# q by Strassen's seven products over two heads and two query blocks, in an attention and gMLP kernel of fp32 products in three passes

## The chip, the cores and the metric

The kernel runs on one core of one Trainium2 chip. The metric is the device time of one execution in microseconds (us). It is told as the median of three runs; one further execution was profiled, and its trace is what the views below read. The engines are PE (TensorE, matrix products into PSUM), DVE (VectorE), ACT (ScalarE), POOL (GpSimd) and SP (SyncE, which here issues most DMAs). Each engine takes its own instructions strictly in the order in which the program wrote them.

## The reference

The input x is 2048 rows of 512. It is normalized per row, and the result feeds an attention with 32 heads over the last 512 cached keys and values (no mask), and a gMLP branch whose SiLU gates the attention's output:

```python
xn = _layernorm(x, axis=-1)
s = _A_ref(xn, A_k_cache, A_v_cache, A_wq, A_wo)   # q = xn @ wq, 32 heads of 128
#   scores = q k^T * 128 ** -0.5 ; p = softmax(scores) ; o = p v ; s = o @ wo
g = _silu(_B_ref(xn, B_w_in, B_w_sp, B_b_sp, B_w_out))
#   z = gelu(xn @ w_in); z1, z2 = halves; z2 = layernorm(z2)
#   (z1 * (w_sp @ z2 + b_sp)) @ w_out
return x + s * g
```

All tensors are fp32.

## The kernel before

Every product is made to hold fp32's accuracy by three passes: an operand is split into a part `hi`, rounded to the matrix engine's fp32r format, and the rest `lo` (the operand minus `hi`), and `mm3` adds hi·hi, hi·lo and lo·hi in PSUM. So each operand costs an ACT instruction (the rounding copy) and a subtraction, `rest`, on DVE or POOL. POOL cannot serve where the operand lies in PSUM; there DVE subtracts.

The work stands in one loop over steps `t` (line 372). A block `b` is one head with 512 queries, so there are 128 blocks of 4 steps; one head takes 16 steps. A step works on several blocks at once, at fixed distances:

- `score(t)`: 3 products of 512 columns into one of four PSUM buffers `ps`, then DVE takes the negated row maximum `nm` (line 229), and ACT writes `prob` = exp(score + nm) with its row sums (line 231). The next-but-one score needs the same PSUM buffer again, so PE can run two steps ahead of ACT's exponential.
- `qproj`, 7 steps ahead: q for a later block, 12 products of 512 columns per block, 3 in each step. At the fourth, ACT and DVE split the result into `qT_h` and `qT_l`.
- `turn(t-1)`: DVE transposes `prob` in 32x32 pieces into `pB` (line 239), SP writes it to a DRAM buffer; two steps after a block's last one `turned` reads it back into `pL` in another order, so that p stands transposed.
- `shares(b, c)`, 10 steps behind: ACT rounds a quarter of `pL` into `pT_h` (line 256), POOL makes the rest `pT_l`.
- `pv`, 12 steps behind: 3 products of p and v per step; after four, ACT and DVE split them into `oT_h` and `oT_l`.
- `outp`, 17 steps behind: 3 products with wo, and DVE scales by the row sum and adds to `sacc` (line 283).

Within a step the engines' orders follow the program: `shares` and the splitting of weights come first, then `score`, then the products, then the splits of results, and `turn` last. So on DVE a step reads `nm`, `sacc`, perhaps `qT_l` and `oT_l`, then `pB`; on ACT it reads `pT_h`, perhaps a weight's rounding, the exponential, then perhaps `qT_h` and `oT_h`.

The weights of a head come in four pieces of 128x512 (wq, k, v, wo), loaded 8 steps before `split_piece` splits them with ACT and POOL. The 32 heads are run one after the other, each over all four query blocks; `sacc` holds all 2048 rows of s. The normalized and transposed x stays on chip as hi and lo (`xh`, `xl`). The first half of the gMLP's input product (`z1_piece`, 12 products of 344 columns each, 32 pieces) fills steps at the start and the end of the loop in which the pipeline is not full. After the loop come the gMLP's second half, the spatial product with w_sp and the last projection, which the change leaves as they are but for buffer names and the order of the row tiles.

Of the kernel before, what the change touches and what calls it, by code (L numbers as in the profile page):

```python
# [17 lines left out]
P = 128  # L18
# [15 lines left out]
XL, QL, ML, PL, OL = 11, 7, 10, 12, 17  # L34
Q = 32
# [3 lines left out]
def mixer_kernel(ctx: ExitStack, tc: tile.TileContext, x, wh, w_in, w_sp, b_sp, w_out, out):  # L39
# [35 lines left out]
    xp = ctx.enter_context(tc.tile_pool(name="xp", bufs=4))  # L75
    wp = left.enter_context(tc.tile_pool(name="wp", bufs=2))
    raws = ExitStack()
    rawp = raws.enter_context(tc.tile_pool(name="rawp", bufs=6))
# [4 lines left out]
    zs = att.enter_context(tc.tile_pool(name="zs", bufs=2))  # L83
    sp = att.enter_context(tc.tile_pool(name="sp", bufs=1))
    ap = att.enter_context(tc.tile_pool(name="ap", bufs=2))
    sacc = sp.tile([P, NT, D], F32, name="sacc")

    raw, wt = {}, {}  # L90

    def load_piece(key, k):
        n = 512 if key[0] == "h" else NB
        r = rawp.tile([P, 512], F32, name="raw")
        raw[key, k] = r
        nc.sync.dma_start(r[:, :n], (wh if key[0] == "h" else w_in)[key[1], :, k])
# [11 lines left out]
    FOLLOWS = {("w", 1): (0, 1, 0, 2), ("w", 2): (1, 3, 2, 3), ("w", 3): (0, 1, 0, 2)}  # L108

    def split_piece(key, k, engine, early=False):  # L110
        n = 512 if key[0] == "h" else NB
        if key == ("w", 0):
            hi = ap.tile([P, 512], F32R, name="pT_h", bufs=4)
            lo = ap.tile([P, 512], F32R, name="pT_l", bufs=4)
        else:
            f = FOLLOWS[key][k] if key in FOLLOWS and not early else k
            hi = wp.tile([P, 512], F32R, name=f"wh{f}")
            lo = wp.tile([P, 512], F32R, name=f"wl{f}")
        r = raw.pop((key, k))[:, :n]
        nc.scalar.copy(hi[:, :n], r)  # L120
# [6 lines left out]
    GROUPS = [(a, a + 1) for a in range(4)] + [(a, a + 2) for a in range(4, NT, 2)]  # L127
    mv, rx, xT = {}, {}, {}
# [4 lines left out]
    def ln_stats(i):  # L133
        a, b = next(g for g in GROUPS if g[0] <= i < g[1])
        if i == a:
            mv[a] = stats.tile([P, 2, 2], F32, name="mv", bufs=5)
        stt = stats.tile([P, 6], F32, name="stt", bufs=4)
        nc.vector.bn_stats(stt, sacc[:, i, :])
        nc.vector.bn_aggr(mv[a][:, i - a, :], stt)
        if i == b - 1:  # L140
            r = stats.tile([P, 2], F32, name="rs_r", bufs=5)
            rsqrt(mv[a][:, :b - a, 1], r, b - a, stats.tile([P, 2], F32, name="rs_t", bufs=4))
            for j in range(a, b):
                rx[j] = mv[a][:, j - a, 0:1], r[:, j - a:j - a + 1]

    def ln_apply(i):
        mean, r = rx[i]
        if i:
            nc.vector.scalar_tensor_tensor(sacc[:, i, :], sacc[:, i, :], mean, r.to_broadcast([P, D]),
                                           op0=OP.subtract, op1=OP.mult)  # L150
        else:
            for k in range(2):
                sl = sacc[:, i, k * (D // 2):(k + 1) * (D // 2)]
                nc.vector.tensor_scalar(sl, sl, mean, r, op0=OP.subtract, op1=OP.mult)

    def ln_flip(i, parts=1):
        g, j = divmod(i, 4)
        if j == 0:
            hi = xp.tile([P, NC, 512], F32R, name="xh")
            lo = xp.tile([P, NC, 512], F32R, name="xl")  # L160
            xT[g] = (hi, lo)
        ps = ps_step.tile([P, NC, P], F32, name="ps_3")
        n, rests = NC // parts, []
        for k in range(parts):
            for c in range(k * n, k * n + n):
                nc.tensor.transpose(ps[:, c, :], sacc[:, i, c * P:(c + 1) * P], ident)  # L166
            hi, lo = (t[:, k * n:k * n + n, j * P:(j + 1) * P] for t in xT[g])
            nc.scalar.copy(hi, ps[:, k * n:k * n + n])
            rests.append((lo, ps[:, k * n:k * n + n], hi))
        return rests if parts > 1 else [rest(nc.vector, *r) for r in rests]  # L170


    def zmm(ps, i, n, cs):
        g, j = divmod(i, 4)
        for c in cs:
            mm3(ps, c == 0, c == NC - 1, tuple(t[:, c, j * P:(j + 1) * P] for t in xT[g]),
                cols(wt[("w", n), c], 0, NB))
# [5 lines left out]
    def zmm_in(order, ps, i, n):  # L183
        g, j = divmod(i, 4)
        for k, (a, b, c) in enumerate(order):
            nc.tensor.matmul(ps, xT[g][a][:, c, j * P:(j + 1) * P], wt[("w", n), c][b][:, :NB],
# [9 lines left out]
    def z1_out(i, n, ps):  # L196
        z = zs.tile([P, 384], F32, name="z1")[:, :NB]
# [8 lines left out]

    def qproj(b, c):
        h, qb = divmod(b, NQ)
        if c == 0:
            qps[b] = ps_acc.tile([P, 512], F32, name="ps_a")  # L210
        mm3(qps[b], c == 0, c == NC - 1, cols(wt[("h", h), 0], c * P, (c + 1) * P), tuple(t[:, c, :] for t in xT[qb]))

    def qproj_out(b, c):
        if c == NC - 1:
            hi = ap.tile([P, 512], F32R, name="qT_h")
            lo = ap.tile([P, 512], F32R, name="qT_l")
            ps = qps.pop(b)
            nc.scalar.activation(hi, ps, AF.Copy, scale=SCALE)
            nc.vector.scalar_tensor_tensor(lo, ps, SCALE, hi.bitcast(F32), op0=OP.mult, op1=OP.subtract)
            qT[b] = (hi, lo)  # L220

    def score(t):
        b, j = divmod(t, 4)
        ps = ps_step.tile([P, W], F32, name="ps_3")
        mm3(ps, True, True, cols(qT[b], j * P, (j + 1) * P), wt[("h", b // NQ), 1])
# [34 lines left out]
    def pv(b, c):  # L260
        if c == 0:
            pps[b] = ps_acc.tile([P, 512], F32, name="ps_a")
        mm3(pps[b], c == 0, c == 3, cols(wt[("h", b // NQ), 2], c * P, (c + 1) * P), pT.pop((b, c)))
# [10 lines left out]
    def outp(b, j):  # L274
        h, qb = divmod(b, NQ)
        i = qb * 4 + j
        ps = ps_step.tile([P, D], F32, name="ps_3")
        mm3(ps, True, True, cols(oT[b], j * P, (j + 1) * P), wt[("h", h), 3])
        rs = sums[b][:, j:j + 1]
        if h == 0:  # L280
            nc.vector.tensor_scalar(sacc[:, i, :], ps, rs, None, op0=OP.mult)  # L281
        else:
            nc.vector.scalar_tensor_tensor(sacc[:, i, :], ps, rs, sacc[:, i, :], op0=OP.mult, op1=OP.add)  # L283
        if h == H - 1:
            nc.sync.dma_start(s_dram[:, i, :], sacc[:, i, :])


    T0, T1, Z1 = -QL, NSTEP + OL, NSTEP - 3
    loads, splits = {}, {}

    def plan(key, k, t):

        loads.setdefault(max(T0, t - 8), []).append((key, k))
        splits.setdefault(t, []).append((key, k))

    for h in range(1, H):
        for k, d in enumerate((-10, -4, 1, 9)):
            plan(("h", h), k, 16 * h + d)
    for k, d in enumerate((-5, 6, 9)):
        splits.setdefault(d, []).append((("h", 0), 1 + k))  # L300
    for n, ds in enumerate(((-12, -9, -7, -4), (1, 4, 13, 17), (17, 17, 17, 17))):
        for k, d in enumerate(ds):
            plan(("w", 1 + n), k, NSTEP + d)
# [7 lines left out]
    load_piece(("h", 0), 0)  # L311
    load_x(4, 8)
    for k in range(1, 4):
        load_piece(("h", 0), k)
    for a in range(8, NT, 4):
        load_x(a, a + 4)
# [12 lines left out]
    ln_stats(0)  # L329
    low0 = split_piece(w0, 0, None), split_piece(w0, 1, None)  # L330
    ln_stats(1)
    ln_apply(0)
# [3 lines left out]
    ln_apply(1)  # L336
    for r in low:
        rest(nc.vector, *r)
    split_piece(w0, 2, nc.vector)
    split_piece(w0, 3, nc.vector)  # L340
# [4 lines left out]
    ln_stats(2)  # L345
# [4 lines left out]
    ln_stats(3)  # L350
# [340 lines left out]
```

## Time and profile before

| | us |
|---|---|
| runs before | 1840.91, 1840.68, 1837.23; median 1840.68 |
| the profiled execution | 1841.09, of which its span 1839.2 |
| loop: score of the first step to that of the last | 45.5 to 1434 (starts, view of `qT_l`'s products) |
| share of the loop in the span | about three quarters |

The span is the time from the first to the last instruction of the trace; 1.9 us lie around it. In the timeline a row has the start in us, the length in us, the engine, the line, the operation, what it writes and reads with shapes, and in brackets how long the engine sat idle ahead of it and who ended that. In the table of windows the columns are the window, its length, then the busy time and the number of instructions of PE, PE's weight loads, DVE, ACT and POOL, then PE's clock, the DMA share and GB/s.

### The profile page before, as it was taken

How to read it: one execution, taken by the hardware profiler on the slowest of the kernel's cores; microseconds unless marked ns; L12 is line 12 of the kernel's file. 1: busy time of each engine (PE TensorE's matmuls, PEld its weight loads, DVE VectorE, ACT ScalarE, POOL GpSimd, SP SyncE). 2: the span in 40 equal slices, each digit the busy share in tenths (PEclk: the TensorE clock that was granted, in tenths of full speed). 3: DMA queues.
4: the chain of work that ended last, by engine and by line, in shares of the span. 5: the costliest groups of instructions: out<-in, count | busy, mean ns of one | idle time of the engine just before them, and what ended most of it. 6: DMA issues, size and time to landing. Idle time of an engine off the chain costs nothing.

```text
span 1839.2 us, 27426 instructions
## 1 busy us (share of the span) xinstructions
PE 1827.4 (99%) x8828; PEld 1573.1 (86%) x8828; DVE 1356.3 (74%) x2268; ACT 1019.4 (55%) x2188; POOL 873.6 (48%) x703
## 2 busy tenths in 40 slices
PE   8999999999999999999999999999999999999999
PEld 7888888888888888888888888888888999999998
DVE  7688888888888888888888888888888566333433
ACT  3566656666666665666666665665666445343422
POOL 3365555565565565555566555565566244000000
PEclk9999999999999999999999999999999999999999
DMA  5698888888888888888888888888888714554532
GB/s 190 179 234 216 217 219 224 215 218 218 221 214 217 216 219 217 216 214 217 219 224 217 218 216 226 215 218 217 218 215 225 222 65 153 174 184 140 182 120 91
DMA packets 404225, 369.69 MB, mean 201 GB/s; under 512 B 23056, under 2 KB 298768, under 8 KB 404080
## 3 DMA queue, kind: packets, MB, share of 16 engines
q1 hardware_dynamic: 399472, 362.30, 75.1%
q10 hardware_dynamic: 4608, 5.64, 0.9%
q8 instruction: 69, 1.13, 0.3%
q14 instruction: 76, 0.62, 0.1%
HBM read 213.70 MB, written 154.14 MB: 200 GB/s over the span
## 4 chain that ended last, share of the span: by engine, by line
PE 96%; DVE 1%; DMA 1%; ACT 1%; issue 0%; POOL 0%; ACTq 0%; SPq 0%; DVEq 0%; POOLq 0%
PE ps_a L61 14%; PE ps_a L62 14%; PE ps_a L63 14%; PE ps L63 13%; PE ps L61 13%; PE ps L62 13%; PE ps_g L61 4%; PE ps_g L62 4%; PE ps_g L63 4%; PE ps_f L63 1%; PE ps_f L62 1%; PE ps_f L61 1%; DMA z_dram<-z 0%; PE ps_f L621 0%; PE ps L166 0%
## 5 line engine op out<-in xcount | busy, mean ns | idle before, releaser
L57 POOL TENSOR_TENSOR pT_l<-pL,pT_h 128x512 fp32r<-128x512 f32 x507 | 658.6, 1299 | 572.1 <-ACT pT_h L256 526.2
L231 ACT ACTIVATE prob<-ps,nm 128x512 f32<-128x512 f32 x512 | 353.4, 690 | 533.6 <-DVE nm L229 531.5
L283 DVE SCALAR_TENSOR_TENSOR sacc<-ps,sums,sacc 128x512 f32<-128x512 f32 x496 | 370.7, 748 | 170.5 <-PE ps L63 170.4
L239 DVE STREAM_TRANSPOSE pB<-prob 128x512 f32<-128x512 f32 x512 | 359.4, 702 | 1.5 <-ACT pT_h L256 0.8
L229 DVE TENSOR_REDUCE nm<-ps 128x1 f32<-128x512 f32 x512 | 334.8, 654 | 3.6 <-PE ps L63 3.6
L256 ACT CAST pT_h<-pL 128x512 fp32r<-128x512 f32 x512 | 315.8, 617 | 7.6 <-ACT z L198 3.4
L61 PE MATMUL ps<-wh,qT_h 128*128 128x512 f32 x512 | 199.9, 390 | 0.9 <-DVE sacc L281 0.9
L63 PE MATMUL ps<-wh,oT_l 128*128 128x512 f32 x512 | 199.3, 389 | 0.3 <-DVE oT_l L57 0.3
L61 PE MATMUL ps_a<-xh,wh 128*128 128x512 f32 x512 | 199.4, 390 | 0.0
L62 PE MATMUL ps_a<-pT_l,wh 128*128 128x512 f32 x512 | 199.3, 389 | 0.0
L62 PE MATMUL ps_a<-xl,wh 128*128 128x512 f32 x512 | 199.3, 389 | 0.0
L62 PE MATMUL ps<-wl,qT_h 128*128 128x512 f32 x512 | 199.3, 389 | 0.0
L63 PE MATMUL ps_a<-xh,wl 128*128 128x512 f32 x512 | 199.2, 389 | 0.0
L63 PE MATMUL ps<-wh,qT_l 128*128 128x512 f32 x512 | 199.2, 389 | 0.0
L62 PE MATMUL ps<-wl,oT_h 128*128 128x512 f32 x512 | 199.2, 389 | 0.0
L61 PE MATMUL ps_a<-pT_h,wh 128*128 128x512 f32 x512 | 199.2, 389 | 0.0
L63 PE MATMUL ps_a<-pT_h,wl 128*128 128x512 f32 x512 | 199.2, 389 | 0.0
L61 PE MATMUL ps<-wh,oT_h 128*128 128x512 f32 x512 | 199.2, 389 | 0.0
L57 POOL TENSOR_TENSOR wl<-raw,wh 128x512 fp32r<-128x512 f32 (+1 forms) x132 | 169.6, 1286 | 37.0 <-ACT wh L120 37.0
L63 PE MATMUL ps_g<-z_h,xl 128*128 128x344 f32 x512 | 161.8, 316 | 0.0
L61 PE MATMUL ps_g<-z_h,xh 128*128 128x344 f32 x512 | 161.8, 316 | 0.0
L62 PE MATMUL ps_g<-z_l,xh 128*128 128x344 f32 x512 | 161.8, 316 | 0.0
(135 smaller groups left out, 2991.4 us busy)
## 6 DMA issues: line engine op xcount, KB each, us to landing
p_dram<-pB SPq DMA_DIRECT2D x512, 256.0 KB, 3.8
pL<-p_dram SPq DMA_DIRECT2D x512, 256.0 KB, 5.8
raw<-wh SPq DMA_DIRECT2D x128, 256.0 KB, 4.4
xh<-w_sp SPq DMA_DIRECT2D x32, 256.0 KB, 5.8
xl<-w_sp SPq DMA_DIRECT2D x28, 256.0 KB, 5.8
u_dram<-uB SPq DMA_DIRECT2D x15, 384.0 KB, 2.3
uL<-u_dram SPq DMA_DIRECT2D x60, 96.0 KB, 2.1
z_dram<-z ACTq DMA_DIRECT2D x32, 172.0 KB, 2.4
```

Source lines behind the costliest of these rows:

```text
L57: engine.tensor_tensor(lo, whole, hi.bitcast(F32), op=OP.subtract)
L61: nc.tensor.matmul(ps, lh, rh, start=first, stop=False)
L62: nc.tensor.matmul(ps, lh, rl, start=False, stop=False)
L63: nc.tensor.matmul(ps, ll, rh, start=False, stop=last)
L229: nc.vector.tensor_reduce(nm, ps, axis=AX.X, op=OP.max, negate=True)
L231: nc.scalar.activation(prob[t], ps, AF.Exp, bias=nm, accum_out=sums[b][:, j:j + 1])
L239: nc.vector.transpose(pB.rearrange("p (k q) -> p k q", q=Q), prob.pop(t))
L256: nc.scalar.copy(h, p)
L283: nc.vector.scalar_tensor_tensor(sacc[:, i, :], ps, rs, sacc[:, i, :], op0=OP.mult, op1=OP.add)
```

## The change

For each pair of heads and pair of query blocks the change computes q by the seven products of Strassen's scheme (in Winograd's form) in place of eight: the two-by-two blocks are (two heads) x (two halves of the 512 inputs) on the weight's side, and (two halves of the inputs) x (two blocks of 512 queries) on x's side. A group `g` is such a pair of pairs: four blocks, 16 steps. Each of its seven products is 6 matmuls of 512 columns, so a group has 42 in place of 48. The first group is computed as before.

What comes with it:

- Four sums of x's blocks per half of the rows ("T1" to "T4") are formed, split into hi and lo, and kept in SBUF beside the original blocks. With them only one half of x fits, so the 32 heads are run twice: first all heads over rows 0 to 1023, then all heads over rows 1024 to 2047 (`where`). `sacc` shrinks to half. k, v and wo are loaded and split twice.
- The first half's sums are made in steps -3 to 1 (`t_sums`, `t_split`). Its original blocks are written to DRAM (`keep_x`) and read back for the stage after the loop. The second half's x is loaded, normalized, transposed, summed, split and written to DRAM in 72 small pieces of work (`later_x`) spread over steps 30 to 207, and fetched as seven blocks of 1 MB (`fetch_x`) while the last group of the first half goes on.
- Per group: two loads of wq, four sums of 128x256 on POOL (`q_sum`), seven splits of 128x256 (`q_split`): ACT rounds each, POOL makes the rest of three, DVE that of four. The products accumulate in three PSUM buffers; ACT evicts three times into `qs`, DVE adds three more results onto these (`q_evict`), and four splits give `qT_h`, `qT_l` (`q_done`): three with ACT and POOL, one with ACT and DVE.
- The z1 pieces stand otherwise: 11 of them in steps -7 to 5 (before: 13 in -7 to 9), and 16 at the end (before: 14).

```diff
+    def q_split(g, k):
+        a11, a12, a21, a22, s1 = q_parts(g)
+        src = (a11, a12, a11, s1, a21, a12, a22)[k]
...
+        nc.scalar.copy(hi, src)
+        rest(nc.gpsimd if k in (0, 1, 5) else nc.vector, lo, src, hi)
...
+    def q_products(g, s):
+        for m in q_span(g, s):
+            k, r = divmod(m, 6)
+            c, v = divmod(r, 3)
+            bank = BANK[k]
...
+            nc.tensor.matmul(qps[g, bank], wt["q", g, k][a][:, c * P:(c + 1) * P], X[g * 2 // H][ORDER[k]][:, b, c],
+                             start=first, stop=r == 5, skip_group_check=True)
+    def q_evict(g, k):
+        ps = qps[g, BANK[k]]
+        if k in (0, 2, 3):
+            t = qps[g, "t", k] = ap.tile([P, 512], F32, name="qs", bufs=3)
+            nc.scalar.activation(t, ps, AF.Copy, scale=SCALE)
+        elif k < 6:
+            t = qps[g, "t", {1: 0, 4: 3, 5: 2}[k]]
+            nc.vector.scalar_tensor_tensor(t, ps, SCALE, t, op0=OP.mult, op1=OP.add)
+    def q_done(g, k):
+        if k == 6:
+            q_out(4 * g + 3, qps[g, "a"], True, nc.vector)
+        else:
+            t, n = {1: (0, 0), 4: (3, 2), 5: (2, 1)}[k]
+            q_out(4 * g + n, qps[g, "t", t], False, nc.gpsimd)
...
+    for h in range(2 * H):
+        for k, d in ((1, -4 if h else -5), (2, 6), (3, 11)):
+            if h:
+                plan(("h", h), k, 8 * h + d)
...
+        t0 = 16 * g - LEAD
+        sums_at, splits_at = (-5, -4, -2, 1), (-3, -1, 2, 4, 6, 7, 10)
...
+    for n, f in enumerate(f for p in range(4) for f in later_x(p)):
+        at(30 + 5 * n // 2, f)
```

In `later_x` each of the four rounds does, in this order: load, statistics of two tiles and two normalizing multiplications on DVE, two transposes on PE with a copy by ACT, four subtractions on POOL, and eight splits of 128x256 of which ACT rounds all, DVE makes the rest of five and POOL that of three; each split is written to DRAM.

DVE in the middle of the loop, before: from one row maximum to the next but two (`oT_l` and `qT_l` are the rests of o and q, `pB` the turned probabilities). Every subtraction here has an operand in PSUM.

```order
L229 TENSOR_REDUCE nm<-ps_8587 128x1
L283 SCALAR_TENSOR_TENSOR sacc<-ps_8601,sums,sacc 128x512
L57 TENSOR_TENSOR oT_l<-ps_a,oT_h 128x512
L239 STREAM_TRANSPOSE pB<-prob 128x512
L229 TENSOR_REDUCE nm<-ps_8621 128x1
L283 SCALAR_TENSOR_TENSOR sacc<-ps_8637,sums,sacc 128x512
L219 SCALAR_TENSOR_TENSOR qT_l<-ps_a,qT_h 128x512
L239 STREAM_TRANSPOSE pB<-prob 128x512
L244 RECIPROCAL sums<-sums 128x4
L229 TENSOR_REDUCE nm<-ps_8654 128x1
```

The same engine with the change, in steps 3 to 6 of a group's products (`x_739` is the ring of split weights, `wq` and `wqs` hold the weights and a sum of them, `qs` the evicted products).

```order
L439 TENSOR_REDUCE nm<-ps_11457 128x1
L494 SCALAR_TENSOR_TENSOR sacc<-ps_11471,sums,sacc 128x512
L449 STREAM_TRANSPOSE pB<-prob 128x512
L59 TENSOR_TENSOR x_739<-wqs,x_739 128x256
L439 TENSOR_REDUCE nm<-ps_11493 128x1
L494 SCALAR_TENSOR_TENSOR sacc<-ps_11507,sums,sacc 128x512
L423 SCALAR_TENSOR_TENSOR qs<-ps_a,qs 128x512
L59 TENSOR_TENSOR oT_l<-ps_a,oT_h 128x512
L449 STREAM_TRANSPOSE pB<-prob 128x512
L439 TENSOR_REDUCE nm<-ps_11526 128x1
L494 SCALAR_TENSOR_TENSOR sacc<-ps_11541,sums,sacc 128x512
L59 TENSOR_TENSOR x_739<-wq,x_739 128x256
```

A subtraction whose two operands both lie in SBUF now stands directly ahead of a row maximum, in four steps of every sixteen.

ACT with the change, from the exponential of step 3 to that of step 6.

```order
L441 ACTIVATE prob,sums<-ps_11457,nm 128x512
L466 CAST pT_h<-pL 128x512
L395 CAST x_739<-wqs 128x256
L441 ACTIVATE prob,sums<-ps_11493,nm 128x512
L480 CAST oT_h<-ps_a 128x512
L466 CAST pT_h<-pL 128x512
L441 ACTIVATE prob,sums<-ps_11526,nm 128x512
L349 CAST qT_h<-qs 128x512
L466 CAST pT_h<-pL 128x512
L395 CAST x_739<-wq 128x256
L441 ACTIVATE prob,sums<-ps_11560,nm 128x512
```

The rounding that DVE's subtraction needs (`x_739`) stands behind the exponential of the step before, the evictions of that step and the rounding of p; before the change, what stood there on ACT beside p was only the rounding of `qT_h`, `oT_h` or of a weight whose rest POOL makes.

More of the change, by code (lines that the diff above doesn't have):

```diff
@@ L274, in outp @@
     def outp(b, j):
-        h, qb = divmod(b, NQ)
+        h, qb = where(b)
         i = qb * 4 + j
+        at = sacc[:, i % T8, :]
         ps = ps_step.tile([P, D], F32, name="ps_3")
@@ L296, in mixer_kernel @@
[L296 to L301, printed above, removed]
-        for k, d in enumerate(ds):
-            plan(("w", 1 + n), k, NSTEP + d)
+        if h % H == 0:
+            nc.vector.tensor_scalar(at, ps, rs, None, op0=OP.mult)
+        else:
+            nc.vector.scalar_tensor_tensor(at, ps, rs, at, op0=OP.mult, op1=OP.add)
@@ L310, in mixer_kernel @@
     load_early(1, [(0, 4)])
-    load_piece(("h", 0), 0)
+    load_piece(("q", 0), 0)
     load_x(4, 8)
[L313 to L316, printed above, removed]
+    load_piece(("h", 0), 1)
+    load_piece(("q", 1), 0)
     ident = const.tile([P, P], F32, name="ident")
@@ L328, in mixer_kernel @@
     w0, w1 = ("w", 0), ("w", 1)
[L329 to L332, printed above, removed]
+    rows = [sacc[:, i, :] for i in range(T8)]
+    ln_open(0)
+    low0 = split_piece(w0, 0, None, True), split_piece(w0, 1, None, True)
+    ln_open(1)
+    ln_apply(rows[0], 0)
     low = ln_flip(0, 2)
@@ L478, in mixer_kernel @@
     SP = (6, 8, 10, 12)
-    for i in range(NT):
+    for pos, i in enumerate(ZO):
         for n in (2, 3):
```

448 lines of the change are left out of this document (320 added, 128 removed).

## The prediction, made before the changed kernel ran

> **What bounds the kernel now.** I read the page's sums first, then the chain that ended last, then a window in the middle of the loop, then the timeline there.
>
> ```profile
> span 1839.2 us, 27426 instructions
> PE 1827.4 (99%) x8828; PEld 1573.1 (86%) x8828; DVE 1356.3 (74%) x2268; ACT 1019.4 (55%) x2188; POOL 873.6 (48%) x703
> PE 96%; DVE 1%; DMA 1%; ACT 1%; issue 0%; POOL 0%; ACTq 0%; SPq 0%; DVEq 0%; POOLq 0%
> 400.00:800.00 400.00, 400.00 (x1767) 331.31 (x1766) 331.79 (x551) 244.33 (x551) 236.11 (x184) 1.00 0.86 218
> ```
>
> PE is busy for 99% and makes 96% of the last chain. In the window DVE is busy for 83%, ACT for 61%, POOL for 59%, with a DMA share of 0.86. The busy PE could still be waiting inside its pipeline, so I look at starts:
>
> ```profile
> 800.16 0.39 PE L61 MATMUL ps<-wh,qT_h 128*128 128x512 f32 x1
> ...
> 800.72 0.74 DVE L283 SCALAR_TENSOR_TENSOR sacc<-ps,sums,sacc 128x512 f32<-128x512 f32 x1
> ...
> 801.38 0.70 DVE L239 STREAM_TRANSPOSE pB<-prob 128x512 f32<-128x512 f32 x1
> ...
> 802.88 0.39 PE L61 MATMUL ps<-wh,qT_h 128*128 128x512 f32 x1
> ```
>
> A step takes 2.72 us for 12 matmuls: 0.2267 us each, though one is shown as 0.39 long. Sixteen steps take 43.5. PE sets the pace; the others have a sixth of the time or more to spare. But PE can run only two steps ahead of the exponential, so what decides after a cut of PE's work is how fast DVE and ACT can go round: row maximum, exponential, further work, next row maximum. The trace shows that once, at the loop's start, where steps are short because `pv` and `outp` have not begun:
>
> ```profile
> 87.57 0.65 DVE L229 TENSOR_REDUCE nm<-ps 128x1 f32<-128x512 f32 x1
> ...
> 88.32 0.69 ACT L231 ACTIVATE prob<-ps,nm 128x512 f32<-128x512 f32 x1 [0.21 <-DVE nm L229]
> ...
> 89.00 0.58 ACT L270 CAST oT_h<-ps_a 128x512 fp32r<-128x512 f32 x1
> ...
> 89.61 0.69 DVE L57 TENSOR_TENSOR oT_l<-ps_a,oT_h 128x512 fp32r<-128x512 f32 x1 [1.38 <-ACT oT_h L270]
> ...
> 90.84 0.65 DVE L229 TENSOR_REDUCE nm<-ps 128x1 f32<-128x512 f32 x1
> ...
> 92.27 0.59 ACT L218 ACTIVATE qT_h<-ps_a 128x512 fp32r<-128x512 f32 x1
> ...
> 92.75 0.62 ACT L256 CAST pT_h<-pL 128x512 fp32r<-128x512 f32 x1
> ...
> 93.25 0.63 ACT L120 CAST wh<-raw 128x512 fp32r<-128x512 f32 x1
> 93.44 1.30 POOL L57 TENSOR_TENSOR pT_l<-pL,pT_h 128x512 fp32r<-128x512 f32 x1 [1.98 <-ACT pT_h L256]
> ...
> 94.18 0.66 DVE L229 TENSOR_REDUCE nm<-ps 128x1 f32<-128x512 f32 x1
> ...
> 95.55 0.50 PE L61 MATMUL ps<-wh,qT_h 128*128 128x512 f32 x1 [0.89 <-DVE sacc L281]
> ...
> 96.03 0.65 DVE L229 TENSOR_REDUCE nm<-ps 128x1 f32<-128x512 f32 x1
> ...
> 97.88 0.65 DVE L229 TENSOR_REDUCE nm<-ps 128x1 f32<-128x512 f32 x1
> ```
>
> Here the round is late and PE waits for it, at 95.55. From one `nm` to the next a late round takes 3.27 us with an `oT` split (87.57 to 90.84), 3.34 with a `qT` split (90.84 to 94.18), 1.85 without (96.03 to 97.88). In the kernel before, sixteen steps hold four of the first, four of the second, eight of the third: 41.2 us, under PE's 43.5. So the round never rules there, with only 5% of room.
>
> **The change part by part.** *PE's work.* 31 groups lose 6 matmuls each: 186 x 0.2267 = 42.2 us. A group's PE time falls from 43.5 to 42.16. Sixteen transposes are added at the start; four take 0.65 us, so 2.6:
>
> ```profile
> 26.92 0.65 PE ps L166 x4
> ```
>
> *The round with the change.* I go through the sixteen steps of a group, `s` = 0 to 15 from its first product, by the rows above. From `nm` to the exponential 0.75 (87.57 to 88.32), from the exponential to ACT's next 0.68 (88.32 to 89.00), then 0.48 for an eviction (92.27 to 92.75) and 0.50 for a rounding of 512 (92.75 to 93.25); the rest on DVE starts 0.03 after its rounding ends (89.00 + 0.58, 89.61). Not shown is a split of 128x256. Its nearest rows:
>
> ```profile
> L120 ACT CAST pT_h<-pL x4: 475/478/482, 4.9 to 9.1; 128x344 fp32r<-128x344 f32 x4
> L57 DVE TENSOR_TENSOR xl<-ps,xh x17: 415/686/693, 9.3 to 58.6; 128x512 fp32r<-128x512 f32 x15, 128x256 fp32r<-128x256 f32 x2
> 1477.12 2.21 DVE L57 TENSOR_TENSOR wl<-raw,wh 128x344 fp32r<-128x344 f32 x5
> ```
>
> Between 0.48 for 344 columns and 0.62 for 512, a rounding of 256 is 0.40. DVE's subtraction of 256 lasts 0.415; of 344 columns five in a row take 0.44 each, so 256 cost 0.35 of DVE's time. An eviction on DVE costs what `sacc` does, 0.66 (800.72 to 801.38). The intervals from `nm` to `nm` when late:
>
> - six plain ones: 11.1; three with `oT`: 9.8; `oT` behind a rounding of `qT_h` (s = 12): 3.27 + 0.50 = 3.77; two with an eviction on DVE (11, 13): 2 x 2.51 = 5.0;
> - 1 to 2, the split of q, then DVE's weight split: 3.34 + 0.35 = 3.7;
> - 3 to 4: 0.75 + 0.68 + 0.50 (p's rounding) + 0.43 + 0.35 = 2.71; 5 to 6 and 9 to 10, with one more instruction on ACT ahead: 3.2 each, 6.4;
> - 2 to 3: eviction, p and a weight piece between two exponentials make ACT later than DVE: 0.4.
>
> Sum 42.9 us. This is above PE's 42.16: the new round replaces PE as what sets the pace, and of 1.36 us per group at most 0.6 are left.
>
> *DVE against POOL.* DVE's four weight splits read two operands from SBUF, which no DVE instruction in the middle of the loop before does. The trace has such a one beside a POOL subtraction:
>
> ```profile
> 1452.06 1.29 POOL L57 TENSOR_TENSOR pT_l<-pL,pT_h 128x512 fp32r<-128x512 f32 x1 [4.96 <-ACT pT_h L256]
> ...
> 1452.40 1.32 DVE L57 TENSOR_TENSOR wl<-raw,wh 128x344 fp32r<-128x344 f32 x1 [1.61 <-ACT wh L120]
> ```
>
> DVE's took 1.32 in place of 0.44 to 0.5, and ended 0.37 after POOL's end: it waited POOL out. In the four steps POOL starts p's subtraction 0.69 after p's rounding (92.75 to 93.44), and DVE becomes ready 0.50 + 0.43 = 0.93 after it. POOL then has 1.05 of 1.29 left: a wait of up to 1.05 at s = 4 and 10, and about 0.55 at s = 2 and 6, where other work delays DVE. Bounds for a group: no wait, 42.9; all waits whole, 46.1. POOL is busy with 25 subtractions of 1.29 and 7 half ones, at some 0.75 (estimated between its 344 and 512 columns, 0.93 and 1.30, in the row below), 37.5 us of every group, so DVE seldom finds it idle, but it may come late in POOL's instruction. I take the middle, 44.5.
>
> ```profile
> L57 POOL TENSOR_TENSOR wl<-raw,wh x132: 927/1300/1307, 34.8 to 1472.8; 128x512 fp32r<-128x512 f32 x127, 128x344 fp32r<-128x344 f32 x5
> ```
>
> The Trainium skill ("SBUF — State Buffer", section "SBUF: two separate sides") calls what DVE and GpSimd share an exclusive lock, held for the whole instruction by whoever starts first, against a DVE op with two SBUF inputs. Taken strictly, each of the four waits is whole and the group is at 46.1, some 48 us more in all than the middle; the row at 1452.40 agrees, but is one case with an otherwise idle POOL.
>
> Over 30 groups (the first one's products lie in the short steps): 30 x (44.5 - 43.5) = +30 us, bounds -18 and +78.
>
> *The second half's x*, in steps 30 to 207. It was made in the start before, where DVE had room; now it stands ahead of `nm` inside the round. Four times: two statistics and two multiplications on DVE, five DVE splits:
>
> ```profile
> L138 DVE BATCH_NORM_STATS2 stt<-sacc x16: 660/684/695, 3.2 to 44.2; 128x6 f32<-128x512 f32 x16
> L149 DVE SCALAR_TENSOR_TENSOR sacc<-sacc,mv,rs_r x15: 720/742/981, 8.7 to 53.7; 128x512 f32<-128x512 f32 x15
> ```
>
> Statistics with their small second step 1.5, multiplications 2 x 0.67, splits between 0.35 and 0.9 more than a plain step, 5 x 0.45: 5.1 us, four times 20. The multiplications and splits have two SBUF operands again; seven waits of 0.6 add up to 17: between 20 and 37, taken 28.
>
> *Start, switch and DMA.* Five steps at the start lose the z1 piece that covered them (12 matmuls of 344, 1.89 us) while the first p is under way; nothing lost or 5 x 1.89 = 9.4, taken 4 with the transposes. At the switch seven loads of 1 MB meet p's traffic:
>
> ```profile
> 15.00:20.00 5.00, 3.46 (x19) 2.88 (x18) 3.88 (x6) 1.01 (x3) 3.87 (x6) 0.90 1.06 396
> pL<-p_dram SPq DMA_DIRECT2D x512, 256.0 KB, 5.8
> ```
>
> At the 396 GB/s of the start's loads 1.05 MB take 2.65 us: seven, at most 18.5 us of delay. But each has two to three steps to itself and p's read lands in 5.8 us, with four steps from its issue to its use: 3 taken. In the loop transfers of 256 KB go from 36 to 40 per group; 0.86 x 40/36 = 0.96 of DMA share at the old pace, 0.93 at the new one: no bound, but little room. Rounding of k, v and wo a second time, and the sums, lie on ACT and POOL between exponentials; what of it is on the round is counted above.
>
> Sum: 1839.2 + 30 + 28 + 4 + 3 = 1904 us of span, with 1.9 around it (the profiled execution's 1841.1 against its span) 1906. The median before lies 0.4 under the profiled execution, which I leave out.
>
> **The rivals.** *PE stays the bound.* The two steps of PE's lead absorb the late rounds, as DVE's mean load would allow (331.8 of 400 now). Then the 42.2 come off, 2.6 and some 10 for start, switch and the x work come on: span 1809, time 1811. For it: PE lost only 0.89 us in the one place shown. Against: the sum of the round, which no lead can shorten. *No meeting with POOL.* DVE comes after POOL's instruction each time: 1839 - 18 + 20 + 7 = 1848, time 1850; against it POOL's 37.5 us of work per group. *Half and half.* PE rules outside the x work (19 groups, 26 gained), the round inside (11 groups at 42.9 and 20 of x work, 13 lost), start and switch 7: 6 gained, time 1835. *DMA becomes the bound*: with 32 writes of 256 KB in short rows and the loads of x the share passes 1 in steps 30 to 207, `pL` lands late, ACT's rounding waits and the exponential behind it. If a tenth is added to those 180 steps (490 us) on top of the forecast: 1955.
>
> **How the numbers follow.** Chances: the forecast 0.47 (its own range 1870 to 1960), PE stays the bound 0.20, no meeting 0.15, half and half 0.12, DMA 0.06. From these: faster 0.24 (the second case and a third of half and half), within 0.2%, about what this measurement can tell from no change, 0.06, slower 0.70. The range must reach into the case of PE's bound and to DMA's: 1812 to 1960 leaves out half of the first, and the ends of the forecast and of DMA, under 0.2 together.
>
> **What would show it.** If the forecast holds, the 16 steps of a group in the second half take 44 to 45.5 us, PE shows gaps ahead of the scores that end on ACT's exponential or on DVE, DVE's `x<-wq` subtractions last about 0.9 on the mean in place of 0.415, and groups in steps 30 to 207 take 2 to 3 us more. PE at 98% or more, groups of 42.2 us and short subtractions would make it wrong; so would POOL or `pL` as the releaser ahead of PE's products, or of ACT's rounding of p.

## The result, and the profile after

| | before | after |
|---|---|---|
| median of 4 runs, us | 1840.22 | 1985.03 (1982.25 to 1987.7) |
| span of the profiled execution, us | 1839.2 | 1982.1 |

The ratio is 1.079, with a 95% interval from 1.077 to 1.081: slower, as forecast, but by 145 us where 66 were forecast, and beyond the range (1812 to 1960). The page's sums and the engines' shares of the chain that ended last, after:

```profile
span 1982.1 us, 28951 instructions
PE 1860.5 (94%) x8658; PEld 1537.5 (78%) x8658; DVE 1484.3 (75%) x2427; ACT 1174.1 (59%) x2627; POOL 1264.1 (64%) x1127
PE 36%; ACT 20%; DVE 17%; DMA 11%; issue 10%; POOL 4%; SPq 1%; ACTq 0%; DVEq 0%; POOLq 0%
```

PE has 170 matmuls fewer in the records and is shown busier than before (1860.5 us for 1827.4), so its busy time does not tell how much it gets done. What tells is the chain: PE fell from 96% to 36%, and ACT and DVE, 1% each before, hold 37%. Two stretches of the table of windows, the first while the second half's x is made, the second behind the switch:

```profile
400.00:800.00 400.00, 361.50 (x1509) 279.87 (x1508) 334.57 (x539) 256.07 (x601) 310.61 (x276) 0.99 0.90 234
1000.00:1400.00 400.00, 385.37 (x1641) 303.55 (x1641) 344.89 (x566) 271.38 (x635) 325.51 (x282) 1.00 0.92 233
```

No engine is full: PE makes 1509 matmuls in the first and 1641 in the second, against 1767 in 400 us before. Its clock is no reason, at 1.00 in the second. What is left is a chain across engines that is full on none. The view of waits says which (us in total, times, longest), first before, then after:

```profile
ACT prob L231 <- DVE nm L229: 531.5, 472, 2.1
...
DVE sacc L283 <- PE ps L63: 170.4, 359, 1.7
```

```profile
ACT prob L441 <- DVE nm L439: 502.7, 328, 7.3
...
PEld ps L63 <- DVE sacc L494: 159.1, 177, 6.5
...
PE ps L63 <- DVE sacc L494: 93.4, 126, 6.1
```

ACT's exponential waits for `nm` in both kernels, before even longer, so this row alone says nothing. What has turned round is PE and DVE: before, DVE's `sacc` waited for PE's product 359 times; now PE's score waits for `sacc`, which DVE makes right behind `nm`. One turn of this round, from the timeline of a steady group, with the rows of other work left out:

```profile
1227.18 0.41 ACT L395 CAST x<-wq 128x256 fp32r<-128x256 f32 x1
1227.49 0.70 DVE L449 STREAM_TRANSPOSE pB<-prob 128x512 f32<-128x512 f32 x1
1228.09 0.75 POOL L386 TENSOR_TENSOR wq<-wq 128x256 f32<-128x256 f32 x1
1228.18 0.95 DVE L59 TENSOR_TENSOR x<-wq,x 128x256 fp32r<-128x256 f32 x1
1228.79 1.48 POOL L59 TENSOR_TENSOR pT_l<-pL,pT_h 128x512 fp32r<-128x512 f32 x1
1229.05 0.68 DVE L439 TENSOR_REDUCE nm<-ps 128x1 f32<-128x512 f32 x1
1229.65 0.74 DVE L494 SCALAR_TENSOR_TENSOR sacc<-ps,sums,sacc 128x512 f32<-128x512 f32 x1
1229.83 0.69 ACT L441 ACTIVATE prob<-ps,nm 128x512 f32<-128x512 f32 x1 [2.24 <-DVE nm L439]
1230.45 0.50 PE L63 MATMUL ps<-wh,qT_h 128*128 128x512 f32 x1 [0.38 <-DVE sacc L494]
```

The weight's rest on DVE starts 0.09 us after a POOL instruction, lasts 0.95 and ends 0.29 after POOL's end (1228.84): it waited POOL out. POOL's next, begun while DVE was at it, took 1.48 in place of 1.30. `nm` stands behind it, the exponential had idled 2.24 us for it, and PE's score starts 0.06 after `sacc`.

A wait can also span several POOL instructions. The timeline of the two engines in step 67:

```profile
255.53 1.31 POOL L59 TENSOR_TENSOR pT_l<-pL,pT_h 128x512 fp32r<-128x512 f32 x1
...
256.02 4.25 DVE L59 TENSOR_TENSOR rawx<-rawx 128x256 fp32r<-128x256 f32 x1 [1.19 <-POOL qT_l L59]
...
256.77 0.76 POOL L59 TENSOR_TENSOR x<-wq,x 128x256 fp32r<-128x256 f32 x1
...
257.47 1.30 POOL L59 TENSOR_TENSOR pT_l<-pL,pT_h 128x512 fp32r<-128x512 f32 x1
...
258.70 1.29 POOL L59 TENSOR_TENSOR wl<-raw,wh 128x512 fp32r<-128x512 f32 x1
```

A subtraction of 0.42 us takes 4.25: it ends 0.28 after the fourth POOL instruction in a row.

**Where the 143 us of span went.** The starts of `nm` in DVE's timeline give each step's length; sixteen steps from step 16g + 3 on are group g. Mean us of a group (the runs are those of the next section):

| | group 1 | 2 to 12 | 13 to 16 (switch) | 17 to 30 | time, us |
|---|---|---|---|---|---|
| before | 42.8 | 43.5 | 43.5 | 43.5 | 1840 |
| after | 57.9 | 50.2 | 47.5 | 45.5 | 1985 |
| PSUM operand on DVE | 57.4 | 49.0 | 47.3 | 43.7 | 1950 |
| rest behind `nm` | 59.3 | 48.7 | 47.2 | 44.7 | 1956 |
| no second half of x | 51.6 | 45.5 | 47.7 | 45.8 | 1933 |
| no writes of x | 59.5 | 50.0 | 47.7 | 45.7 | 1989 |
| all on POOL | 54.8 | 47.4 | 46.3 | 42.9 | 1908 |
| copies in PSUM | 56.2 | 48.7 | 47.7 | 45.1 | 1962 |
| copies, `oT` later | 51.9 | 46.2 | 48.2 | 42.9 | 1902 |
| everything together | 45.1 | 45.4 | 47.0 | 42.3 | 1870 |
| the same, no x | 42.2 | 42.4 | 46.1 | 42.5 | 1835 |
| the same, no writes | 44.7 | 42.9 | 46.1 | 42.2 | 1838 |
| the same, rows of 2 KB | 43.8 | 43.4 | 46.1 | 42.4 | 1851 |

Against before, the change loses 5.0 us until group 1 begins, 15.1 in group 1, 73.7 in groups 2 to 12, 15.8 in 13 to 16, 27.8 in 17 to 30, and 5.3 at the end.

### The profile page after: what moved, and what is told of

Its sections match the earlier page's. It is cut to its first block, busy times and chain, and to the rows that moved or that the text cites. A ratio compares the mean times of both kernels' runs of the same rounds, so it can differ in the third digit from the quotient of the medians.

```text
span 1982.1 us, 28951 instructions
## 1 busy us (share of the span) xinstructions
PE 1860.5 (94%) x8658; PEld 1537.5 (78%) x8658; DVE 1484.3 (75%) x2427; ACT 1174.1 (59%) x2627; POOL 1264.1 (64%) x1127
## 4 chain that ended last, share of the span: by engine, by line
PE 36%; ACT 20%; DVE 17%; DMA 11%; issue 10%; POOL 4%; SPq 1%; ACTq 0%; DVEq 0%; POOLq 0%
ACT prob L441 8%; DVE nm L439 6%; ACT pT_h L466 4%; DMA pL<-p_dram 4%; PE ps_g L64 4%; PE ps_g L63 4%; PE ps_g L65 4%; DVE pB L449 4%; PE ps L63 3%; PE ps L65 3%; PE ps L64 3%; PE ps_a L413 3%; PE ps_a L64 3%; PE ps_a L63 3%; PE ps_a L65 3%
## 5 line engine op out<-in xcount | busy, mean ns | idle before, releaser
L59 POOL TENSOR_TENSOR pT_l<-pL,pT_h 128x512 fp32r<-128x512 f32 x507 | 670.7, 1323 | 266.9 <-ACT pT_h L466 244.5
L413 PE MATMUL ps_a<-x,x 128*128 128x512 f32 x1302 | 383.5, 395 | 0.5 <-DVE oT_l L59 0.3
L494 DVE SCALAR_TENSOR_TENSOR sacc<-ps,sums,sacc 128x512 f32<-128x512 f32 x496 | 363.4, 733 | 17.7 <-PE ps L65 16.6
L466 ACT CAST pT_h<-pL 128x512 fp32r<-128x512 f32 x512 | 317.3, 620 | 23.7 <-DMA pL<-p_dram 10.6
L63 PE MATMUL ps<-wh,qT_h 128*128 128x512 f32 x512 | 221.8, 433 | 97.5 <-DVE sacc L494 92.3
L413 PEld LDWEIGHTS ps_a<-x,x 128*128 128x128 f32 x1302 | 247.7, 190 | 57.0 <-DVE oT_l L59 1.9
L59 POOL TENSOR_TENSOR wl<-raw,wh 128x512 fp32r<-128x512 f32 x192 | 251.6, 1311 | 8.7 <-ACT wh L139 8.7
L63 PEld LDWEIGHTS ps<-wh,qT_h 128*128 128x128 f32 x512 | 96.6, 189 | 180.6 <-DVE sacc L494 155.9
L63 PE MATMUL ps_g<-z_h,x 128*128 128x344 f32 x512 | 162.2, 317 | 0.5 <-ACT z L719 0.5
L64 PE MATMUL ps_g<-z_l,x 128*128 128x344 f32 x512 | 162.1, 317 | 0.4 <-POOL z_l L59 0.4
L65 PE MATMUL ps_g<-z_h,x 128*128 128x344 f32 x512 | 161.9, 316 | 0.0
```

Source lines behind the costliest of these rows:

```text
L59: engine.tensor_tensor(lo, whole, hi.bitcast(F32), op=OP.subtract)
L63: nc.tensor.matmul(ps, lh, rh, start=first, stop=False)
L64: nc.tensor.matmul(ps, lh, rl, start=False, stop=False)
L65: nc.tensor.matmul(ps, ll, rh, start=False, stop=last)
L413: nc.tensor.matmul(qps[g, bank], wt["q", g, k][a][:, c * P:(c + 1) * P], X[g * 2 // H][ORDER[k]][:, b, c], start=first, stop=r == 5, skip_ ...
L466: nc.scalar.copy(h, p)
```

## The experiments

The last two kernels were run four times; the others once, next to a run of the kernel before on the same chip (1839.3 to 1841.3 us). The four runs of the changed kernel lie within 0.3%, which is enough for steps of 20 us and more. Of each edit the main lines are shown.

### Is it the meeting with POOL?

DVE's four weight splits get one operand from PSUM.

```diff
-        rest(nc.gpsimd if k in (0, 1, 5) else nc.vector, lo, src, hi)
+        if k in (0, 1, 5):
+            rest(nc.gpsimd, lo, src, hi)
+        else:
+            nc.vector.tensor_tensor(lo, src, kept[0], op=OP.subtract)
```

> The four weight splits of a group that are on DVE subtract a constant tile in PSUM in place of the rounded part in SBUF: the same operation and length, one SBUF operand fewer; the low part of these weights is then not what the reference needs. Theory (DVE's instruction with two SBUF operands waits until POOL's instruction has ended, and this wait stands ahead of nm in the round): x<-wq on DVE falls to 0.42 us, a group of the second half from 45.3 to about 42.7 (the measured waits are 0.51 + 0.78 + 0.40 + 0.89 = 2.6), and the time by 75 to 85 us to 1900 to 1910. Rival (the split's place ahead of nm costs, whatever it reads): under 10 us, 1975 to 1985.

1949.6 us. Groups of DVE's instructions by line, after, then in this run (count, then busy time and mean ns of one):

```profile
L59 DVE TENSOR_TENSOR x<-wq,x 128x256 fp32r<-128x256 f32 x93 | 95.6, 1028 | 57.3 <-ACT x L395 57.3
...
L59 DVE TENSOR_TENSOR x<-wqs,x 128x256 fp32r<-128x256 f32 x31 | 26.9, 867 | 24.5 <-ACT x L395 24.5
```

```profile
L400 DVE TENSOR_TENSOR x<-wq,warm 128x256 fp32r<-128x256 f32 x93 | 36.0, 387 | 0.0
...
L400 DVE TENSOR_TENSOR x<-wqs,warm 128x256 fp32r<-128x256 f32 x31 | 11.9, 383 | 0.0
```

The same operation on the same columns goes from 122.5 us in all to 47.9, and none of the 124 is longer than 0.40 us. Place and operation are the same, so the extra length belongs to the second SBUF operand. By the Trainium skill ("SBUF — State Buffer", section "SBUF: two separate sides"), a DVE operation with two SBUF inputs and a GpSimd operation that reads SBUF exclude each other for the whole instruction; these two rows agree.

But the run changes two things more. The subtraction does not read the rounded part, so it no longer waits for ACT's rounding either (57.3 and 24.5 us of idle time, now 0.0), and the constant takes one of the four PSUM buffers `ps`. The intervals that end at s = 4, 6 and 10 (steps of the group's products, as in the prediction) fall to 2.16, 2.21 and 2.21 us, below the 2.71, 3.2 and 3.2 of the prediction's round without any meeting. So the time of this run does not price the meeting. The lengths do: with the change the four subtractions of a group last 1.03, 0.86, 0.80 and 1.32 us on the mean of groups 17 to 30, together 2.5 us more than four of 0.39.

The time fell by 35 us and not by 75 to 85. Groups 17 to 30 came near the expected 42.7 at their best (42.8 to 43.1 in five of the fourteen), but by luck: PE sets the pace there (it sat idle for only 4.5 us between 830 and 1400 us), and not the round without its waits. On the mean they take 43.7, since `pL` now lands late at times, which was not in the expectation (ACT waits 31.8 us for it in that stretch, 2.9 without the edit). Groups 2 to 12 hardly moved, and the x work's own splits go on waiting there (1.19 us on the mean).

### Or its place ahead of `nm`?

```diff
-        rest(nc.gpsimd if k in (0, 1, 5) else nc.vector, lo, src, hi)
+        if k in (0, 1, 5):
+            rest(nc.gpsimd, lo, src, hi)
+        else:
+            late.setdefault(t, []).append((rest, (nc.vector, lo, src, hi)))
...
             score(t)
+        for f, args in late.pop(t, ()):
+            f(*args)
```

> The four weight splits of DVE keep their operands and their roundings on ACT keep their place, but DVE does them right behind the step's nm in place of ahead of it. Theory (the round from nm by the exponential and ACT's roundings to the next nm sets the pace, DVE's time as such does not): the steps with a split lose it and its wait (0.9 + 1.2 + 0.8 + 1.3 = 4.2 us), until PE is the bound: a group of the second half 42.2 to 42.9, the time lower by 70 to 90 us, 1895 to 1915. Rival (DVE and POOL meet as often, and DVE has no time left): group 44.5 to 45.3, time within 20 us of 1985.

1956.4 us, between the two. The steps with a split give 6.4 us (their sum goes from 15.5 to 9.1 in groups of the second half), and the steps right behind them take 5.5 back (8.9 to 14.4 for s = 3, 5, 7 and 11). The wait stands in DVE's order wherever it is put, and was even longer here; the timeline of one of its three longest:

```profile
1025.60 5.17 DVE L59 TENSOR_TENSOR x<-wq,x 128x256 fp32r<-128x256 f32 x1
1030.69 0.74 DVE L497 SCALAR_TENSOR_TENSOR sacc<-ps,sums,sacc 128x512 f32<-128x512 f32 x1
```

So my expectation was wrong that DVE has the time once `nm` is first: what is saved ahead of one `nm` is lost ahead of `sacc` and the next.

### The second half's x: engines or DMA?

```diff
-    for n, f in enumerate(f for p in range(4) for f in later_x(p)):
-        at(30 + 5 * n // 2, f)
```

> The second half's x is not made: the work on rows 1024 to 2047 of x in steps 30 to 207 is left out, and the blocks fetched at the switch are copies of the first half's. Theory (this work takes its time inside the round, measured as 67 us against the pace of the second half, most of it waits of DVE for POOL): the groups in steps 19 to 208 go from a mean of 50.1 to 45.3 to 46, the time by 60 to 70 us to 1915 to 1925. Rival (the prediction's term): 28 us, 1957. Rival (the load on DMA of the whole loop): under 15 us.

1932.5 us: 52 less. Group 1 gives 6.3 and groups 2 to 12 give 52.0 together, 58 against the 28 predicted; the start and groups 13 to 30 take some 7 of it back. Group 1 stays at 51.6: something else is in it.

```diff
-            nc.sync.dma_start(xd[1, k][:, :, :, p * P:(p + 1) * P],
-                              st.bitcast(F32).rearrange("p (a c q) -> p a c q", a=2, q=P))
```

> The second half's x is made but not written to DRAM (32 writes of 256 KB are left out; the blocks fetched at the switch are copies of the first half's). Theory (DVE's instructions and their waits for POOL cost the 67 us): under 15 us, 1970 to 1985. Rival (the writes hold SP's queue and the DMA ahead of p's): 30 to 60 us, 1925 to 1955.

1989.3 us, no gain at all, though the DMA share in 400 to 800 us falls from 0.90 to 0.85:

```profile
400.00:800.00 400.00, 361.61 (x1506) 280.79 (x1506) 337.09 (x536) 255.28 (x598) 309.93 (x275) 0.98 0.85 220
```

Both times DVE is busy for 84%. So the writes are not what costs here, and the work on the engines is left. DVE's part of it, in the changed kernel: the 20 splits last 1.27 us on the mean in place of 0.42 (17 us in all), and the statistics wait for the load that was issued two to three steps ahead (8.7):

```profile
L59 DVE TENSOR_TENSOR rawx<-rawx 128x256 fp32r<-128x256 f32 x20 | 25.4, 1268 | 10.7 <-ACT rawx L267 8.1 <-POOL wq L386 1.3 <-POOL qT_l L59 1.2
...
L171 DVE BATCH_NORM_STATS2 stt<-rawx 128x6 f32<-128x512 f32 x8 | 5.4, 680 | 8.7 <-DMA rawx<-x 8.6
```

### Two ways round the meeting

POOL alone makes all these rests:

```diff
-        rest(nc.gpsimd if k in (0, 1, 5) else nc.vector, lo, src, hi)
+        rest(nc.gpsimd, lo, src, hi)
...
-        vec, gp = nc.vector, nc.gpsimd
+        vec, gp = nc.gpsimd, nc.gpsimd
```

> All subtractions with two operands in SBUF go to POOL: the four weight splits of a group that DVE has, and the 20 of the second half's x. Theory (what costs is DVE's wait behind POOL's instructions, whose queue it enters only when POOL pauses): DVE has no such wait left; groups 17 to 30 at 42.8 to 44, set by PE (42.2 at a clock of 0.985) and now and then by a late pL; groups 2 to 12 at 43 to 45; the time 1870 to 1895. Rival (POOL, with 4 x 0.75 us more on a queue of 37.5 per group, becomes late and PE waits for pT_l or for a weight): groups of 45 and more, with POOL as releaser ahead of PE's matmuls, the time 1930 or more.

1907.6 us, 77 less, the largest step of all. The theory's groups 17 to 30 came out (42.9); 2 to 12 stayed above it (47.4), and with them the time. They gained 2.8 each, hardly more than the 2.6 of the later groups, though the splits of x went to POOL as well: another bound stands there, which comes below. Together with the meeting this edit takes DVE's instruction and its wait for ACT's rounding out of the round.

Or ACT puts a copy of the weight into PSUM a step ahead, so that DVE subtracts with a real operand from there:

```diff
+        if early:
+            wpsum[g, k] = halves_p[0][:, k % 2]
+            return nc.scalar.copy(wpsum[g, k], src)
...
+            rest(nc.vector, lo, wpsum.pop((g, k)), hi)
```

> ACT copies each of the four weights that DVE splits to PSUM a step ahead of its split, and DVE subtracts with that operand from PSUM: nothing of the result changes, ACT has four instructions of 0.41 us more per group. The second half's x is split by POOL alone. Theory: x<-wq on DVE falls to 0.4 us as with the constant tile, groups 17 to 30 at 42.8 to 44.5, groups 2 to 12 at 43 to 45.5, the time 1875 to 1900. Rival (ACT, with 1.6 us more per group inside the round, takes back what the wait gives): groups 17 to 30 at 44.5 to 45.3, the time 1920 or more.

1962.4 us: the rival. The meeting is gone, with the rounding still waited for: the 124 subtractions take 0.39 to 0.43 us. (The copies take one of the four buffers `ps`, here and in the next run.) ACT's 1.6 us stand in the round and take back what the wait gave: 45.1. If so, work that is taken out of the round must give it again. In the next run the rest of o, which idles on DVE for `oT_h` ahead of `nm`, comes behind the next `nm`:

```diff
-            rest(nc.vector, lo, ps, hi)
+            late.setdefault(4 * b + PL + 4, []).append((rest, (nc.vector, lo, ps, hi)))
             oT[b] = (hi, lo)
```

> As the run with the copies in PSUM, and besides the statistics of the second half's x come two items (5 steps) later behind their load, and DVE's subtraction for oT stands behind the nm of the next step. Theory (in a round what DVE does between the exponential and the next nm counts): the three late steps with oT go from 3.3 to about 2.7, so that PE rules everywhere but in the x work: groups 17 to 30 at 42.7 to 43.5, the time 15 to 30 us under the run with the copies alone. Rival (PE or the DMA sets the pace there already): within 8 us of it.

1902.1 us: 60 less than without it, twice the upper end of what was expected; in groups 17 to 30, which the later statistics do not touch, 2.2 us per group (45.1 to 42.9). Copies, roundings and DVE's work are the same in number; only the order around `nm` is another. That is the round, shown without POOL.

What is left in groups 1 to 16 of this run is another wait, ACT's for `pL`, 60.6 us in 25 waits between 100 and 800 us. The longest:

```profile
146.41 0.61 ACT L350 CAST qT_h<-qs 128x512 fp32r<-128x512 f32 x1
155.12 0.62 ACT L475 CAST pT_h<-pL 128x512 fp32r<-128x512 f32 x1 [8.09 <-DMA pL<-p_dram]
155.64 0.40 ACT L401 CAST x<-wq 128x256 fp32r<-128x256 f32 x1
155.94 0.68 ACT L450 ACTIVATE prob<-ps,nm 128x512 f32<-128x512 f32 x1
```

It stands in group 1: 8 us, behind the three kept blocks of 1 MB written in steps 22 to 28 and the first loads of x.

### What stands behind the round

The next run joins POOL's rests, the later `oT` and statistics, and x's large transfers in pieces:

```diff
+        ends.setdefault(22 + 14 * n, []).append((keep_piece, k, *p))
...
+        for n, p in enumerate(PIECES):
+            ends.setdefault(16 * (NG // 2 - 1) - LEAD + d + 2 * n, []).append((fetch_piece, 1, ORDER[k], *p))
```

> Everything that helped, together: all subtractions with two SBUF operands on POOL, DVE's subtraction for oT behind the nm of the next step, the statistics of x two items after their load, and the 1 MB transfers of x (three kept blocks, seven fetched ones) cut into pieces of 256 KB, 14 steps apart for the kept ones and two steps apart for the fetched ones. Theory: PE rules in groups 17 to 30 (42.0 to 42.6); what is left in groups 1 to 16 is late pL, less of it with the pieces: groups 2 to 12 at 43.5 to 46, 13 to 16 at 44 to 47; the time 1865 to 1888. Rival (the transfers' size is not what makes pL late, their sum is): groups 2 to 16 as in the runs before it, 46 to 48, the time 1888 to 1900.

1870.1 us. Twelve of the groups 17 to 30 take between 42.16 and 42.3: PE's 186 matmuls, the figure that the prediction had worked out. Group 1 falls to 45.1. Groups 13 to 16 stay at 47.0, so cutting the transfers up gains nothing there; that their sum counts is likely, but not shown. The next two runs leave out the x work, then its writes alone.

> The same with the second half's x not made (the blocks fetched are copies of the first half's). Theory (without the meetings with POOL, the x work costs by its 2 MB read and 8 MB written on a DMA that has little room, and by DVE's statistics): groups 2 to 12 at 42.2 to 43, 15 to 40 us under the run with it. Rival (late pL in groups 2 to 12 comes from p's and the weights' own traffic): within 10 us of it.

1835.0 us, 35 less than with the x work, and groups 2 to 12 at 42.4.

> The same as the run with everything together, with the x made but its 32 writes of 256 KB left out. In the kernel as changed these writes cost nothing (1989 without them). Theory (a bound that was behind the round comes forward when the round is short): 8 to 20 us less than the run with everything together. Rival (the writes never matter): within 5 us of it.

1837.9 us: the same writes that cost nothing in the changed kernel cost 32 us here, where 8 to 20 were expected. The prediction's rival of the DMA was wrong for the changed kernel and comes near for what stands behind it: `pL` lands late, at a DMA share of 0.96. Waits of SP's own queue and of ACT in 200 to 600 us, with everything together:

```profile
SPq L277 <- POOL rawx L59: 43.9, 16, 6.4
```

```profile
ACT pT_h L474 <- DMA pL<-p_dram: 62.9, 22, 6.1
```

and in ACT's without the writes:

```profile
ACT pT_h L472 <- DMA pL<-p_dram: 17.6, 16, 2.2
```

A write of x, issued right behind its split, holds SP until POOL's subtraction is done (43.9 us in 16 waits), and p's write and read queue behind it. So the last pair issues the write a step later and stores x in blocks of 128 rows, 2 KB at a piece:

```diff
-            nc.sync.dma_start(xd[1, k][:, :, :, p * P:(p + 1) * P],
-                              st.bitcast(F32).rearrange("p (a c q) -> p a c q", a=2, q=P))
+            ends.setdefault(now[0] + 1, []).append((write, k, st))
+        def write(k, st):
+            nc.sync.dma_start(xd[1, k][:, p], st.bitcast(F32).rearrange("p (a c q) -> p a c q", a=2, q=P))
```

> The run with everything together, and the second half's x in DRAM and SBUF ordered by blocks of 128 rows of x, so that a write of 256 KB has rows of 2 KB in place of four of 512 B, and the write is issued at the end of the next step in place of right behind the split, so that SP's queue does not wait there for POOL's subtraction ahead of p's write. PE's moving operand is then four pieces of 128 columns. Theory (the 32 us that the writes cost are SP's wait and the short rows): half or more of them comes off, groups 2 to 12 at 42.5 to 44, the time 1840 to 1855. Rival (the bytes themselves cost): 1862 to 1872. Rival (PE is slower with a moving operand in four pieces): the groups from 16 on go up, 1 us or more each.

1850.7 us (1848.4 to 1853.5, four runs), 1.0059 times before with an interval from 1.0044 to 1.0074. Some 19 of the 32 us came off, SP's wait on POOL's splits of x falls from 43.9 us to 1.5, and ACT's wait for `pL` in 200 to 600 us is halved:

```profile
ACT pT_h L481 <- DMA pL<-p_dram: 31.9, 21, 3.3
```

Queue and row length were changed together, so their shares are not told apart. PE is no slower with its operand in four pieces (42.16 in ten groups).

```diff
-        at(-3 + p, t_sums, p)
-        at(-2 + p, t_split, p)
+        at(p, t_sums, p)
+        at(1 + p, t_split, p)
```

> The same, and the sums and splits of the first half's T blocks come three steps later (steps 0 to 4 in place of -3 to 1), where POOL and PE are waited for less. Theory (at the start PE waits 3 us for sums that take turns between DVE and POOL): 2 to 5 us less than the run before. Rival (the wait only moves into the short steps at the loop's start, where the round rules): within 2 us of it, or more.

1862.0 us, 11 more: the rival, and worse. The first `nm` comes 5.2 us earlier (49.2 for 54.4), but its next ones now stand behind the sums, which go from DVE to POOL and back. DVE's timeline:

```profile
54.22 0.41 DVE L228 TENSOR_TENSOR sacc<-sacc,ps 128x256 f32<-128x256 f32 x1
56.14 0.42 DVE L231 TENSOR_TENSOR sacc<-ps,sacc 128x256 f32<-128x256 f32 x1 [1.51 <-POOL sacc L230]
56.48 0.68 DVE L454 TENSOR_REDUCE nm<-ps 128x1 f32<-128x512 f32 x1
...
61.02 0.41 DVE L228 TENSOR_TENSOR sacc<-sacc,ps 128x256 f32<-128x256 f32 x1
62.94 0.42 DVE L231 TENSOR_TENSOR sacc<-ps,sacc 128x256 f32<-128x256 f32 x1 [1.52 <-POOL sacc L230]
63.28 0.68 DVE L454 TENSOR_REDUCE nm<-ps 128x1 f32<-128x512 f32 x1
```

A step of 6.8 us (56.48 to 63.28), the same mistake as the change's in small.

No version here that does all the work beats the kernel before. The nearest is 10.6 us behind it. Its profiled execution, 7.5 us longer in span (1846.7), gains 1.1 us in each of groups 17 to 30, 15 in all, and gives back 10 at the switch, 6 until group 1 and 7 behind group 30.

## Why the prediction was right in the direction and wrong in the size

- **PE loses the pace to the round from `nm` to `nm`: right.** The chain, PE's waits for `sacc` and the later `oT` show it. The intervals taken from the loop's start hold: by s, the medians of the second half are 1.85 to 1.89 in plain steps (predicted 1.85), 3.26 to 3.29 with `oT` (3.27), 3.78 at s = 12 to 13 (3.77), 2.45 and 2.50 with an eviction on DVE (2.51). Only the 0.4 from s = 2 to 3 did not come (1.88). Less the waits the group is then 42.7, not 42.9; this is worked out, no run shows it alone. Of the signs named, all came but one: the groups in steps 30 to 207 take 4.7 us more, not 2 to 3.
- **"I take the middle, 44.5": wrong, a term mis-sized.** DVE's four waits are 0.5, 0.8, 0.4 and 0.9 us (what s = 2, 4, 6 and 10 lie above their sums of 3.7, 2.71, 3.2 and 3.2): 2.6 of the 3.2 that were the bound, where the middle is 1.6 (the lengths of the subtractions give 2.5). POOL had nearly always begun when DVE came. "It may come late in POOL's instruction" was set against the only row there was. The middle is 1.0 us below the measured 45.5, the bound with each wait whole 0.6 above it; that bound stood beside the rule of the Trainium skill ("SBUF — State Buffer", section "SBUF: two separate sides"). In groups 17 to 30 this makes 27.8 us in place of 14, over all 30 groups some 60 in place of 30.
- **The x work, "between 20 and 37, taken 28": wrong, 58 by the run without it.** Its waits were at the upper bound (17). Left out was DVE's stop for a load issued two or three steps ahead (8.7), and that a wait can span several POOL instructions (4.25 and 2.77 us in one step each). If the 20 for the work itself hold, about 10 us of the 58 are not assigned.
- **Start 4: right** (5.0). **Switch 3: too little.** Groups 13 to 16 lie 2.0 each above 17 to 30, 8 us, and 15 to 19 in the runs with everything together (46.1 to 47.0 against 42.3), where the round no longer hides it. The reason given was that each fetch "has two to three steps to itself". The DMA has 0.08 left (0.92 in the window from 1000 us), which is the likely cause; no run shows it, and smaller pieces did not help.
- **A term that was missing:** the kept blocks. Their 3 MB are written in steps 22 to 28; group 1 is at 51.6 without the x work, 6 above the second half's pace, and falls from 51.9 to 45.1 in the run where they are spread. What else differs in that run is worth 0.6 in groups 17 to 30; no run spreads the blocks alone.
- **The end** lost 5.3 where nothing was counted. Two more z1 pieces stand there (2 x 1.89 us by the prediction's figure); this was not tried.
- **The sum.** The span came out 78 us above the forecast of 1904. By these figures 30 of them are the pace of the round with its meetings, 30 the x work, 6 the kept blocks, 5 the switch, 5 the end and 1 the start.
- **"PE can run only two steps ahead of the exponential": the reason was wrong.** The score starts 0.06 us behind `sacc` of two steps back (1230.45, and so in 82 of the 224 steps of groups 17 to 30); in 84 of the 224 it starts before that step's exponential ends. No term of the sum rested on it.
- **Rivals.** PE as the bound was excluded rightly; its figure of 42.16 is exact once the meeting is gone and the round is short. The DMA did not rule, and is next in line.

## What to carry to other kernels

When an engine with 99% is relieved by 3%, first add up the chain of waits that comes next, engine by engine in program order, and look at what the relief puts into it: here four subtractions of 0.4 us in sixteen steps, with the wait that each brought, turned a gain of 1.4 us into a loss of 2. A DVE subtraction with both operands in SBUF beside a busy POOL costs its own length and what is left of POOL's instruction; send it to POOL, or take one operand from PSUM if that takes no extra instruction in the same chain. And take a transfer that costs nothing today as free only until the bound ahead of it is lifted.

## What the runs showed of the hardware that was not expected

- Of the changed kernel's 144 subtractions with two SBUF operands on DVE (splits of weights and of x in its timeline, beside POOL's) 134 came in after one POOL instruction and 4 only after three or four in a row; the other six waited under 0.1 us or not at all. Five in a row were waited out by 3 of the run with the rest behind `nm` (5.17 us, 1025.60). What decides which of the two goes next when both wait stays open.
- POOL pays as well: its subtraction of 1.30 us takes 1.47, the median of 90, when it starts while such a subtraction is under way on DVE (1228.79 is one).
- With one operand in PSUM the same subtraction was 0.38 to 0.40 us in all 124 cases (the constant), and 0.39 to 0.43 in all 124 (the copies), with POOL at work as before.
- A matmul whose moving operand is four pieces of 128 columns, 512 elements apart, keeps the pace of a contiguous one (a group at 42.16 in both).
